# Attention and gated FFN in one kernel: two head groups of the second 512 queries taken ahead, K and Q fillers at half the rate, the first FFN 43 steps later

## The chip, the cores and the metric

The kernel runs on one core of a Trainium2 chip. The metric is the time of one execution on the device in microseconds (us), the median of several runs. The core has four engines that matter here: PE multiplies matrices, ACT evaluates functions such as exp, DVE does elementwise work, SP only issues DMAs. Each engine works through its own instructions in program order.

## What is computed

One transformer layer for 2048 tokens of width 512: a layer norm, attention with 32 heads of width 16, a residual add, a second layer norm, and a gated FFN with 1792 hidden units.

```python
qkv = (x @ wqkv).reshape(B, S, 3, H, Dh)            # x is layernorm(A_x); S=2048, H=32, Dh=16
scores = einsum("bhqd,bhkd->bhqk", q, k) * Dh ** -0.5
o = einsum("bhqk,bhkd->bhqd", softmax(scores), v)
h = A_x + o.reshape(B, S, D) @ wo
hn = layernorm(h)
out = h + (sigmoid(hn @ w_gate) * (hn @ w_up)) @ w_down
```

With 32 heads and 2048 x 2048 scores each, 134 million exponentials are needed. They are the largest piece of work.

## The kernel before, in words

**Chunks, groups, units, steps.** The queries are cut into five chunks c: 0, 1 and 2 of 512 queries, 3 and 4 of 256. The 32 heads are cut into eight head groups g of four heads. A pair (c, g) is worked off over all keys before the next one; the list `qgs` is the order of the pairs, before the change simply c by c, and g by g within c. A unit is a tile of 128 keys by 512 queries of one head (two tiles by 256 queries in chunks 3 and 4); a pair (c, g) of chunks 0 to 2 has 64 units. Three units make a step: three score matmuls on PE (L783) write three PSUM banks `pss`, and one exp on ACT (L794, up to 128x1536) reads them and writes a tile `pt`. There are 683 steps, and two `pss` buffers, so the scores of step i+2 wait until step i has been read. A pair takes 21.3 steps, a chunk of 512 queries 170.7 steps.

**Split steps.** In every fourth step from step 8 to step 680 (`split`), ACT takes only two units (128x1024), and DVE computes the third exp by arithmetic on the bits, in five instructions spread over four steps: L813 (which reads `pss`), L816, L819, L822, L826. I call four steps from one split to the next a cycle. In some cycles, listed in `twice`, a second step is split too. A cycle is also the unit of the timetable: the products with V (`emit_pv`, L864) of four steps come together in one step of the next cycle.

**Score forms.** In the first 44 steps, in odd steps and in `twice` cycles the score matmuls use half the rows of the array each, so that two of them can run side by side (`pairs`); where no filler work is near (`idle`) they do not.

**The filler.** Everything else is one long generator, `filler()`, whose matmuls `emit_fill` slips in behind the scores, at a rate per step (`rate`) and with pauses ("gap", "at", "from"). In order: the nine V tiles left over from the prologue (`fill_v`); for b = 1, 2, 3 the K rows of head groups 2b and 2b+1 (`fill_k`) and the Q rows of chunk 0 for the same groups (`fill_q0`); the Q rows of the other queries, 512 at a time (`fill_q`); then for each chunk c the output projection, the layer norm, gate, up and down products (`ffn_tasks`), each started at a step that depends on the end of the chunk's attention. The filler's products go to one PSUM tile `pm`, so the next block can start only when DVE has emptied it. Up to step 44 (`FIRST`) the rate is that of the V tiles, up to 10 matmuls a cycle; after that it is `RATES[0]`, 2, 2, 0 and 3 in the four steps of a cycle, 0 in the step with three V products.

**What limits the order.** A pair (c, g) needs the K rows of group g//2 and the Q rows of its own queries. `emit_q_rows` and `emit_q_bound` fetch the next pair's Q rows with six DMAs on SP, some four steps before the pair starts. SP also carries the K rows to their places (`k_spread`, two DMAs for each b), the weights (`load_w`: w_gate and w_up from step 44 to 79, w_down from step `GM`+21), the sums of the softmax and back (`emit_norm`: ten small DMAs for each pair), the residual rows and the output.

**Buffers with two lives.** `stg` holds K and the squares of the fillers, `wd` the down weights. Up to step `GM`, three of the seven `pt` buffers lie in `wd`; from `GM` on they lie in `stg` and in the Q rows of chunk 0. The scratch of a second split lies in the buffer `OT` that is free at that time.

**Where each piece falls.** Walking the filler by its rates and pauses, step by step, gives for the kernel before:

| piece of the filler | steps |
|---|---|
| V tiles | 1 to 16 |
| K of b = 1, then Q of chunk 0 for b = 1 | 17 to 31 |
| b = 2 | 31 to 56 |
| b = 3 | 56 to 83 |
| Q of queries 512 to 2047 | 83 to 168 |
| FFN of chunk 0: projection and norm / gate and up / down | 187 to 217 / 217 to 273 / 274 to 320 |
| FFN of chunk 1: the same | 359 to 389 / 389 to 445 / 446 to 492 |
| FFN of chunk 2 | from 523 |
| `twice` cycles of chunk 1's steps, by their second split | 226, 242, 258, 274, 290, 302, 314, 326, 338, 350 |
| `twice` cycles of chunk 2's steps | 402, 418, 434, 450, 458, 470, 482, 494, 506, 518 |

Of the kernel before, what the change touches and what calls it, by code (L numbers as in the profile page):

```python
# [18 lines left out]
def kernel(  # L19
# [13 lines left out]
    S, D = A_x.shape[1], A_x.shape[2]  # L33
# [5 lines left out]
    NG = H // 4  # L39
    FC = F // P  # L40
    QC = 512
    TQ = QC // P
    CHUNKS = [(0, QC), (QC, QC), (2 * QC, QC), (3 * QC, QC // 2), (3 * QC + QC // 2, QC // 2)]
    NC = len(CHUNKS)
    NQC = S // QC
    GU = 3
    CYC = 4
    RATES = ((2.0, 2.0, 0.0, 3.0), (2.0, 2.5, 0.0, 3.0))
    FIRST = 44
    GM = 188  # L50
    G1 = 680
    QS = DH ** -0.5 * 1.4426950408889634 * 2.0 ** 23
    LEAD = 0.106445681
# [14 lines left out]
    def pm_tile():  # L68
        return pmh["pool"].tile([P, 512], FP32, name="pm")
# [27 lines left out]
    QTu = const.tile([P, 4, S], BF16)  # L97
# [65 lines left out]
    def qk_mm(ps, part, b, n, c):  # L163
        w0 = part * D + b * P
        nc.tensor.matmul(ps[:], lhsT=wqkv_sb[:, c, w0:w0 + P], rhs=xnT[:, c, n * QC:(n + 1) * QC],  # L165
                         start=(c == 0), stop=(c == DC - 1))

    def norm_mm(ps, b, sq, start=True, stop=True):
        nc.tensor.matmul(ps[:], lhsT=ones_blk[:, b, :, :].rearrange("p r h -> p (r h)"), rhs=sq,
                         start=start, stop=stop)  # L170
# [21 lines left out]
    def q_root(ps, qc):  # L192
        r = slice(32 * qc, 32 * qc + 32)
        sqrt_bits(y0[r, :], ps[r, :])

    def q_bound(qc, add):
        r = slice(32 * qc, 32 * qc + 32)
        y = y0[r, :].bitcast(FP32)
        if add:
            nc.vector.scalar_tensor_tensor(out=bnd[r, :], in0=y, scalar=nks[r, 0:1], in1=bnd[r, :],  # L200
                                           op0=ALU.mult, op1=ALU.add)
        else:
            nc.vector.tensor_scalar(out=bnd[r, :], in0=y, scalar1=nks[r, 0:1], scalar2=None, op0=ALU.mult)
# [8 lines left out]
        copy(out=Vaug[:, t, :, 0:DH], in_=heads(ps[:]))  # L212

    ready = set()
    qgs = [(c, g) for c in range(NC) for g in range(NG)]

    def emit_q_rows(n):
        c, g = qgs[n]
# [173 lines left out]
    def per_bank(c):  # L392
        return QC // CHUNKS[c][1]

    def n_k(c):
        return NT // per_bank(c)

    units = [(c, g, k, j) for c in range(NC) for g in range(NG) for k in range(n_k(c)) for j in range(4)]
    groups = [units[i:i + GU] for i in range(0, len(units), GU)]
    NS = len(groups)  # L400
    SPC = NS / NQC

    def first_step(c):
        return NS * CHUNKS[c][0] / S if c < NC else NS

    def fill_v(t):
        ps = pm_tile()
        for c in range(DC):  # L410
            yield 1
            v_mm(ps, t, c)
        v_store(t, ps, nc.vector.tensor_copy)
        ready.add(("v", t))
        yield ("gap", 0)

    def squares(src):
        sq = work.tile([P, QC], BF16, name="sq", tag="xn")
        nc.vector.tensor_tensor(out=sq[:], in0=src, in1=src, op=ALU.mult)
        return sq  # L420
# [35 lines left out]
    def q_store(dst, ps):  # L456
        nc.vector.tensor_scalar(out=dst, in0=ps[:], scalar1=QS, scalar2=None, op0=ALU.mult)

    def fill_q0(b):
        ps = pm_tile()  # L460
        for c in range(DC):
            yield 1
            qk_mm(ps, 0, b, 0, c)
        q_store(QTu[:, b, 0:QC], ps)
        sq = squares(QTu[:, b, 0:QC])
        yield ("gap", 2)
        pn = pm_tile()
        yield 1
        norm_mm(pn, b, sq[:])
        q_root(pn, 0)  # L470
        q_bound(0, True)
        ready.add(("q", 0, b))
        ready.add(("b", 0, b))
        yield ("gap", 1)

    def fill_q(qc):
        cols = slice(qc * QC, (qc + 1) * QC)
        sq4 = stages[qc % 2]
        for b in range(4):
            ps = pm_tile()  # L480
            for c in range(DC):
                yield 1
                qk_mm(ps, 0, b, qc, c)
            q_store(QTu[:, b, cols], ps)
            nc.vector.tensor_tensor(out=sq4[:, b * QC:(b + 1) * QC], in0=QTu[:, b, cols], in1=QTu[:, b, cols],
                                    op=ALU.mult)
            ready.add(("q", qc, b))
            yield ("gap", 3)
        yield ("gap", 2)
        pn = pm_tile()  # L490
        for b in range(4):
            yield 1
            norm_mm(pn, b, sq4[:, b * QC:(b + 1) * QC], start=(b == 0), stop=(b == 3))
        q_root(pn, qc)
        q_bound(qc, False)
        for b in range(4):
            ready.add(("b", qc, b))
        yield ("gap", 1)

# [242 lines left out]
    def filler():  # L742
        for t in range(NV0, NT):
            yield from fill_v(t)
        for b in range(1, 4):
            yield from fill_k(b)
            yield from fill_q0(b)
        for qc in range(1, NQC):
            yield from fill_q(qc)
        for c in range(NC - 1):  # L750
            yield ("from", int(first_step(c + 1)) + (11 if c + 3 >= NC else 15))
            yield from ffn_tasks(c)
        yield from wo_early(NC - 1)

    def rate(i):
        if i < FIRST:
            rates = (4.0 if i > 5 else 0.0, 4.0 if i < 6 else 2.0 if i > 16 else 0.0, 0.0, 4.0)
        elif i - i % CYC + 2 in twice:
            rates = (2.0, 2.0, 0.0, 3.0)
        else:  # L760
            rates = RATES[i >= 3 * SPC]
        return (rates[i % CYC], 1.0, 1.0, 0.0)[n_pv.get(i, 0)]

    def emit_scores(i):
        group = groups[i]
        n = len(group)
        pss = pss2[(i + 1) % 2]
        idle = i >= 3 * FIRST and (state["done"] or state["wait"] > i + CYC)
        pairs = i < FIRST or (i % 2 == 1 or i - i % CYC + 2 in twice) and not idle
        order = list(enumerate(group))  # L770
        if pairs and group[0][3] // 2 == group[1][3] // 2:
            order[1:] = order[:0:-1]
        n_of = max(per_bank(u[0]) for u in group)
        parts = [(ui, u, h) for h in range(n_of) for ui, u in order[:2] if h < per_bank(u[0])]
        parts += [(ui, u, h) for ui, u in order[2:] for h in range(per_bank(u[0]))]
        for ui, (c, g, k, j), h in parts:
            n_qg = c * NG + g
            w = CHUNKS[c][1]
            kt = k * per_bank(c) + h
            assert ("k", g // 2) in ready  # L780
            h0 = 64 * (j // 2)
            rows = slice(h0, h0 + 64) if pairs else slice(0, P)
            nc.tensor.matmul(pss[:, ui, h * w:(h + 1) * w], lhsT=KT[rows, g, kt * P:(kt + 1) * P],  # L783
                             rhs=QB[n_qg % 2][rows, j, 0:w], start=True, stop=True,
                             tile_position=(h0, 0) if pairs else None)
        for c, g, k, j in group:
            n_qg = c * NG + g
            if k == (12 if per_bank(c) == 1 else 0) and j == 3 and n_qg + 1 < len(qgs):
                emit_q_rows(n_qg + 1)
                emit_q_bound(n_qg + 1)  # L790
        slot = i % 7
        pt = pt4[slot] if slot < 4 else (pt_early if i < GM else pt_late)[slot - 4]
        na = n - 1 if i in split else n
        ex = nc.scalar.activation(out=pt[:, 0:na, :], in_=pss[:, 0:na, :], func=ACT.Exp, scale=DH ** -0.5 / QS)  # L794
        if na < n:
            scratch = scratch_of(i)
            tc.declare_no_dep(exp_bits(pss[:, na, :], *scratch).ins, ex.ins,
                              reason="both only read, from different banks")
            later(i + 1, lambda: exp_first(*scratch))
            later(i + 2, lambda: exp_second(*scratch))  # L800
            later(i + 3, lambda: exp_third(pt[:, na, :], *scratch))
        for ui, u in enumerate(group):
            p_of[u] = pt[:, ui, :]

    def scratch_of(i):
        if i % CYC:
            flat = OT[(int((i - 20) / SPC) + 1) % 2][:].rearrange("p g q -> p (g q)")
            return (flat[:, 0:2 * QC].bitcast(mybir.dt.int32), flat[:, 2 * QC:4 * QC].bitcast(mybir.dt.int32),
                    flat[:, 4 * QC:6 * QC].bitcast(FP32))
        return early_scratch if i < GM else late_scratch  # L810

# [94 lines left out]
    def load_w():  # L906
# [4 lines left out]
        for f in (0, 7):  # L911
            later(GM + 21 + f // 2, lambda f=f: nc.sync.dma_start(out=wd[:, f:f + 7, :], in_=wd_v[:, f:f + 7, :]))

# [2 lines left out]
    split = set(range(8, G1, CYC))  # L916
    twice = set()
    for qc in range(1, NQC):
        n0 = int(qc * SPC) + 52
        for n in range(n0, min(int((qc + 1) * SPC) + 16, int(first_step(NC - 1)) + 14)):  # L920
            if n % ((4 if n < n0 + 56 else 3) * CYC) == 0:
                twice.add(n + 2)
    split |= twice
# [88 lines left out]
```

## Time and profile before

| what | value |
|---|---|
| median of three runs | 966.0 us (963.1 to 966.93) |
| the profiled execution's own time | 962.96 us |
| its span, first to last instruction | 961.1 us |
| first exp of step 0 starts | 34.24 us after the span's start |
| step 17 / 33 / 185 / 525 starts | 59.28 / 81.12 / 269.98 / 707.67 us |
| DVE busy / POOL busy | 788.1 us (82%) / 41.5 us (4%) |

The starts of steps are the starts of the exps L794 in the timeline of ACT, counted from step 0; a cycle's time is the distance between the starts of steps n and n+4. An exp of 128x1536 is listed with about 1.45 us, but the next one starts 1.33 us after it, since neighbours overlap; busy shares of ACT near 100% mean that there is no gap between them.

### The profile page before, as it was taken

The page shows a single profiled execution, that of the slowest core. Times are in us where ns is not written, and L with a number is a line of the kernel's source. Part 1 is how long each engine was busy: PE and PEld are TensorE (multiplying, and loading weights), DVE is VectorE, ACT ScalarE, POOL GpSimd, SP SyncE. Part 2 cuts the span into 40 slices and gives each one's busy share as a digit, 9 for nine tenths or more (in the row PEclk, how much of TensorE's full clock was granted, in tenths as well). Part 3 has the DMA queues.
Part 4 walks back from the last instruction along what each step waited for, and adds up shares of the span by engine and source line. Part 5 has one row for each costly group of instructions (what it writes and reads, how often), then busy time and mean ns, then how long its engine had stood idle before and what let it go on. Part 6 is the DMA issues. An engine that isn't in the chain of part 4 may idle for free.

```text
span 961.1 us, 17150 instructions
## 1 busy us (share of the span) xinstructions
PE 826.7 (86%) x6327; PEld 337.8 (35%) x6425; DVE 788.1 (82%) x1428; ACT 895.3 (93%) x767; POOL 41.5 (4%) x49
## 2 busy tenths in 40 slices
PE   4887888888788999988788999988788999888998
PEld 2322222222222332222222233222355555455646
DVE  8589998888788888899888888888888788777653
ACT  4789999999999999999999999999998999899872
POOL 4700000000000000000000000000000000000000
PEclk9999999999999999999999999999999999999999
DMA  5001350000013000000011000001011000110010
GB/s 160 21 8 50 114 117 17 16 16 2 16 26 103 16 16 17 19 12 26 14 27 26 16 16 15 14 15 26 16 31 23 16 13 13 27 32 16 9 35 12
DMA packets 37500, 28.38 MB, mean 30 GB/s; under 512 B 17708, under 2 KB 32776, under 8 KB 37416
## 3 DMA queue, kind: packets, MB, share of 16 engines
q1 hardware_dynamic: 35828, 25.71, 10.4%
q10 hardware_dynamic: 1588, 1.58, 0.5%
q8 instruction: 50, 0.82, 0.4%
q14 instruction: 34, 0.28, 0.1%
HBM read 20.31 MB, written 2.61 MB: 24 GB/s over the span
## 4 chain that ended last, share of the span: by engine, by line
PE 40%; DVE 26%; ACT 23%; issue 7%; DMA 3%; SPq 1%; ACTq 0%; DVEq 0%; POOL 0%; POOLq 0%
PE pss L783 20%; ACT pt L794 12%; PE acc L864 8%; PE pm L530 6%; ACT stg L794 4%; ACT wd L794 4%; DVE stg L813 3%; ACT QTu L794 2%; PE pm L546 2%; DVE reg L816 2%; DVE st L139 2%; DVE pt L826 2%; DVE y L822 2%; PE pm L506 2%; DVE reg L543 1%
## 5 line engine op out<-in xcount | busy, mean ns | idle before, releaser
L783 PE MATMUL pss<-QB,KT 64*128 64x512 bf16 (+3 forms) x2542 | 475.8, 336 | 86.9 <-ACT pt L794 43.8
L794 ACT ACTIVATE pt<-pss 128x1536 bf16<-128x1536 f32 (+1 forms) x392 | 501.1, 1363 | 16.3 <-PE pss L783 12.0
L783 PEld LDWEIGHTS <-KT 64*128 64x128 bf16 (+1 forms) x2560 | 181.4, 95 | 345.3 <-issue 232.5
L794 ACT ACTIVATE stg<-pss 128x1536 bf16<-128x1536 f32 (+1 forms) x140 | 183.1, 1355 | 4.6 <-PE pss L783 3.8
L813 DVE TENSOR_SCALAR stg<-pss 128x512 int32<-128x512 f32 x123 | 84.8, 689 | 69.3 <-PE pss L783 53.0
L864 PE MATMUL acc<-pt,Vaug 128*17 128x512 bf16 (+1 forms) x1471 | 112.5, 338 | 4.5 <-DVE xs_all L838 3.2
L794 ACT ACTIVATE wd<-pss 128x1536 bf16<-128x1536 f32 (+1 forms) x80 | 103.8, 1390 | 2.7 <-PE pss L783 2.4
L794 ACT ACTIVATE QTu<-pss 128x1024 bf16<-128x1024 f32 (+1 forms) x71 | 95.5, 1345 | 1.7 <-PE pss L783 1.2
L819 DVE SCALAR_TENSOR_TENSOR y<-reg 128x512 f32<-128x512 f32 x123 | 85.2, 692 | 4.2
L822 DVE SCALAR_TENSOR_TENSOR y<-y,reg 128x512 f32<-128x512 f32 x123 | 84.2, 684 | 1.1
L864 PEld LDWEIGHTS <-Vaug 128*17 128x17 bf16 x2560 | 50.4, 89 | 96.1 <-issue 80.8
L530 PE MATMUL pm<-reg,reg 128*128 128x512 bf16 (+1 forms) x252 | 55.6, 333 | 8.7 <-DVE reg L543 6.6
L530 PE MATMUL pm<-reg,wu 128*128 128x512 bf16 (+1 forms) x280 | 58.1, 338 | 1.5 <-ACT sg L535 1.2
L546 PE MATMUL pm<-wd,reg 128*128 128x512 bf16 x173 | 51.2, 381 | 5.7 <-issue 2.9
L146 POOL TENSOR_TENSOR rs<-ve,pw_neg 128x1 f32<-128x1 f32 (+1 forms) x24 | 17.7, 736 | 888.9 <-DVE ve L144 758.0
L816 DVE TENSOR_SCALAR reg<-stg 128x512 int32<-128x512 int32 x123 | 52.0, 423 | 2.0
L864 PE MATMUL acc<-stg,Vaug 128*17 128x256 bf16 (+1 forms) x564 | 50.6, 326 | 0.6 <-DVE stg L826 0.4
L543 DVE SCALAR_TENSOR_TENSOR reg<-sg,pm 128x512 bf16<-128x512 f32 x56 | 38.2, 682 | 13.9 <-PE pm L530 13.5
L826 DVE SCALAR_TENSOR_TENSOR pt<-y,stg 128x512 bf16<-128x512 f32 x70 | 47.8, 683 | 1.8
L535 ACT ACTIVATE sg<-pm 128x512 f32<-128x512 f32 x56 | 35.6, 637 | 10.1 <-PE pm L530 9.8
L813 DVE TENSOR_SCALAR wd<-pss 128x512 int32<-128x512 f32 x45 | 30.9, 688 | 15.9 <-PE pss L783 14.9
L165 PE MATMUL pm<-reg 128*128 128x512 bf16 x112 | 35.6, 391 | 2.2 <-issue 0.8
(129 smaller groups left out, 707.5 us busy)
## 6 DMA issues: line engine op xcount, KB each, us to landing
rb_all<-rd SPq DMA_DIRECT2D x96, 64.0 KB
reg<-in_A_x_dram SPq DMA_DIRECT2D x8, 256.0 KB
xr<-in_A_x_dram SPq DMA_DIRECT2D x16, 128.0 KB
out_dram<-ob SPq DMA_DIRECT2D x15, 128.0 KB
rb_all<-rd SPq DMA_DIRECT2D x60, 32.0 KB
KT<-stg SPq DMA_DIRECT2D x7, 256.0 KB
reg<-in_B_w_gate_dram SPq DMA_DIRECT2D x4, 448.0 KB
wu<-in_B_w_up_dram SPq DMA_DIRECT2D x4, 448.0 KB
```

The costliest lines, as they stand in the source:

```text
L165: nc.tensor.matmul(ps[:], lhsT=wqkv_sb[:, c, w0:w0 + P], rhs=xnT[:, c, n * QC:(n + 1) * QC], start=(c == 0), stop=(c == DC - 1))
L530: nc.tensor.matmul(ps[:, i * w:(i + 1) * w], lhsT=wt[:, c, f * P:(f + 1) * P], rhs=hnT[:, c, 0:w], start=(c == 0), stop=(c == DC - 1))
L543: nc.vector.scalar_tensor_tensor(out=out, in0=a, scalar=1.0, in1=b, op0=ALU.add, op1=ALU.mult)
L546: nc.tensor.matmul(ps[:], lhsT=hT[:, f, tt * P:(tt + 1) * P], rhs=wd[:, f, :], start=(f == 0), stop=(f == FC - 1))
L783: nc.tensor.matmul(pss[:, ui, h * w:(h + 1) * w], lhsT=KT[rows, g, kt * P:(kt + 1) * P], rhs=QB[n_qg % 2][rows, j, 0:w], start=True, stop= ...
L794: ex = nc.scalar.activation(out=pt[:, 0:na, :], in_=pss[:, 0:na, :], func=ACT.Exp, scale=DH ** -0.5 / QS)
L813: return nc.vector.tensor_scalar(out=e_bits, in0=src, scalar1=ONE_BITS, scalar2=0.0, op0=ALU.add, op1=ALU.max)
L816: nc.vector.tensor_scalar(out=e_man, in0=e_bits, scalar1=0x7FFFFF, scalar2=-0x40800000, op0=ALU.bitwise_and, op1=ALU.bitwise_or)
L819: nc.vector.scalar_tensor_tensor(out=e_pol, in0=m, scalar=PA, in1=m, op0=ALU.add, op1=ALU.mult)
L822: nc.vector.scalar_tensor_tensor(out=e_pol, in0=e_pol, scalar=PB, in1=e_man.bitcast(FP32), op0=ALU.add, op1=ALU.mult)
L826: nc.vector.scalar_tensor_tensor(out=dst, in0=e_pol, scalar=PC, in1=e_bits.bitcast(FP32), op0=ALU.add, op1=ALU.mult)
L864: nc.tensor.matmul(acc[32 * j:32 * j + VW, 0:w], lhsT=Vaug[:, kt, 4 * g + j, :], rhs=p[:, h * w:(h + 1) * w], start=(kt == 0), stop=(kt == ...
```

## The change

The order of the pairs becomes (0,0), (0,1), (1,0), (1,1), (0,2) to (0,7), (1,2) to (1,7), and then chunks 2, 3 and 4 as before. Chunk 0 so ends at step 213.3 in place of 170.7, chunk 1 at step 341.3 as before. K of b = 1 is first needed in step 85 in place of 42. The V rate ends at step 24 (`VF`), while 44 (`FIRST`) still rules the score forms, and after it the rates are 2, 1, 0 and 1 in place of 2, 2, 0 and 3. The filler computes Q of the second 512 queries for b = 0 right behind the V tiles; `fill_q` of these queries leaves that block out, and its pause behind each block is 1 step in place of 3. `GM` and with it the change of buffers and the load of w_down come 28 steps later. The starts of the FFNs and of the `twice` cycles go by the step in which a chunk really ends (`end_step`).

```diff
-    RATES = ((2.0, 2.0, 0.0, 3.0), (2.0, 2.5, 0.0, 3.0))
+    RATES = ((2.0, 1.0, 0.0, 1.0), (2.0, 2.5, 0.0, 3.0))
     FIRST = 44
-    GM = 188
+    GM = 216
+    VF = 24
...
-    qgs = [(c, g) for c in range(NC) for g in range(NG)]
+    qgs = [(c, g) for g0, g1 in ((0, 2), (2, NG)) for c in range(2) for g in range(g0, g1)]
+    qgs += [(c, g) for c in range(2, NC) for g in range(NG)]
+    at_qg = {qg: n for n, qg in enumerate(qgs)}
...
-    units = [(c, g, k, j) for c in range(NC) for g in range(NG) for k in range(n_k(c)) for j in range(4)]
+    units = [(c, g, k, j) for c, g in qgs for k in range(n_k(c)) for j in range(4)]
...
-    def first_step(c):
-        return NS * CHUNKS[c][0] / S if c < NC else NS
+    def end_step(c):
+        return (max(n for n, u in enumerate(units) if u[0] == c) + 1) / GU
...
-    def fill_q0(b):
+    def fill_q1(qc, b):
+        cols = slice(qc * QC, (qc + 1) * QC)
...
-        q_bound(0, True)
-        ready.add(("q", 0, b))
-        ready.add(("b", 0, b))
+        q_bound(qc, b > 0)
+        ready.add(("q", qc, b))
+        ready.add(("b", qc, b))
...
-    def fill_q(qc):
+    def fill_q(qc, b0):
...
-        for b in range(4):
+        for b in range(b0, 4):
...
-            yield ("gap", 3)
+            yield ("gap", 1)
...
     def filler():
         for t in range(NV0, NT):
             yield from fill_v(t)
+        yield from fill_q1(1, 0)
         for b in range(1, 4):
             yield from fill_k(b)
-            yield from fill_q0(b)
+            yield from fill_q1(0, b)
         for qc in range(1, NQC):
-            yield from fill_q(qc)
+            yield from fill_q(qc, int(qc == 1))
         for c in range(NC - 1):
-            yield ("from", int(first_step(c + 1)) + (11 if c + 3 >= NC else 15))
+            yield ("from", int(end_step(c)) + (11 if c + 3 >= NC else 15))
             yield from ffn_tasks(c)
...
     def rate(i):
-        if i < FIRST:
+        if i < VF:
...
-        n0 = int(qc * SPC) + 52
-        for n in range(n0, min(int((qc + 1) * SPC) + 16, int(first_step(NC - 1)) + 14)):
+        n0 = int(end_step(qc - 1)) + 52
+        for n in range(n0, min(int((qc + 1) * SPC) + 16, int(end_step(NC - 2)) + 14)):
```

The same walk for the changed order gives these steps:

| piece of the filler | steps before | steps after |
|---|---|---|
| V tiles | 1 to 16 | 1 to 16 |
| Q of the second 512 queries, b = 0 | in the 83 to 168 below | 17 to 23 |
| K and Q of b = 1 | 17 to 31 | 23 to 51 |
| K and Q of b = 2 | 31 to 56 | 51 to 83 |
| K and Q of b = 3 | 56 to 83 | 83 to 113 |
| the rest of Q | 83 to 168 | 113 to 181 |
| FFN of chunk 0: projection and norm / gate and up / down | 187 to 217 / 217 to 273 / 274 to 320 | 231 to 261 / 261 to 317 / 318 to 364 |
| FFN of chunk 1: the same | 359 to 389 / 389 to 445 / 446 to 492 | 371 to 401 / 401 to 457 / 458 to 504 |
| FFN of chunk 2 | from 523 | from 523 |
| `twice` of chunk 1's steps | 226, 242, 258, 274, 290, 302, 314, 326, 338, 350 | 274, 290, 306, 322, 326, 338, 350 |
| `twice` of chunk 2's steps | ten, from 402 to 518 | the same |

More of the change, by code (lines that the diff above doesn't have):

```diff
@@ L462, in fill_q0 @@
             yield 1
-            qk_mm(ps, 0, b, 0, c)
-        q_store(QTu[:, b, 0:QC], ps)
-        sq = squares(QTu[:, b, 0:QC])
+            qk_mm(ps, 0, b, qc, c)
+        q_store(QTu[:, b, cols], ps)
+        sq = squares(QTu[:, b, cols])
         yield ("gap", 2)
@@ L469, in fill_q0 @@
         norm_mm(pn, b, sq[:])
-        q_root(pn, 0)
-        q_bound(0, True)
-        ready.add(("q", 0, b))
-        ready.add(("b", 0, b))
+        q_root(pn, qc)
+        q_bound(qc, b > 0)
+        ready.add(("q", qc, b))
+        ready.add(("b", qc, b))
         yield ("gap", 1)
-    def fill_q(qc):
+    def fill_q(qc, b0):
         cols = slice(qc * QC, (qc + 1) * QC)
         sq4 = stages[qc % 2]
-        for b in range(4):
+        for b in range(b0, 4):
             ps = pm_tile()
@@ L487, in fill_q @@
             ready.add(("q", qc, b))
-            yield ("gap", 3)
+            yield ("gap", 1)
         yield ("gap", 2)
         pn = pm_tile()
-        for b in range(4):
+        for b in range(b0, 4):
             yield 1
-            norm_mm(pn, b, sq4[:, b * QC:(b + 1) * QC], start=(b == 0), stop=(b == 3))
+            norm_mm(pn, b, sq4[:, b * QC:(b + 1) * QC], start=(b == b0), stop=(b == 3))
         q_root(pn, qc)
-        q_bound(qc, False)
-        for b in range(4):
+        q_bound(qc, b0 > 0)
+        for b in range(b0, 4):
             ready.add(("b", qc, b))
@@ L776, in emit_scores @@
         for ui, (c, g, k, j), h in parts:
-            n_qg = c * NG + g
+            n_qg = at_qg[c, g]
             w = CHUNKS[c][1]
@@ L786, in emit_scores @@
         for c, g, k, j in group:
-            n_qg = c * NG + g
+            n_qg = at_qg[c, g]
             if k == (12 if per_bank(c) == 1 else 0) and j == 3 and n_qg + 1 < len(qgs):
```

## The prediction

> **What bounds the kernel now.** First the page: which engine is nearest to full.
>
> ```profile
> PE 826.7 (86%) x6327; PEld 337.8 (35%) x6425; DVE 788.1 (82%) x1428; ACT 895.3 (93%) x767; POOL 41.5 (4%) x49
> PEclk9999999999999999999999999999999999999999
> ```
>
> ACT, mostly with exps, and the clock of PE is full everywhere. Averages hide stages, so next the busy time by stage: the last V tiles and the first K (steps 17 to 32), the other K and Q fillers (33 to 184), the FFN of chunk 0 in its down part (273 to 320), the steps without filler behind it (321 to 356), the down part of chunk 1 (445 to 492).
>
> ```profile
> core 0: us, PE busy (x) PEld busy (x) DVE busy (x) ACT busy (x) POOL busy (x), PEclk, DMA share, GB/s
> 59.30:81.10 21.80, 18.36 (x122) 5.04 (x122) 20.32 (x42) 20.26 (x16) 0.00 (x0) 1.00 0.11 26
> 81.10:270.00 188.90, 155.62 (x1005) 48.75 (x1023) 160.63 (x283) 188.57 (x154) 0.00 (x0) 1.00 0.17 44
> 386.80:445.60 58.80, 53.20 (x340) 16.61 (x345) 53.13 (x90) 58.34 (x49) 0.00 (x0) 1.00 0.08 20
> 445.60:490.30 44.70, 34.49 (x212) 11.48 (x216) 39.46 (x67) 44.29 (x38) 0.00 (x0) 1.00 0.09 22
> 607.00:668.00 61.00, 52.70 (x340) 16.21 (x345) 53.66 (x91) 58.78 (x50) 0.00 (x0) 1.00 0.08 19
> ```
>
> The reader is to see that where the K and Q fillers run, ACT is idle for 0.33 us of 188.9. The fillers that the change slows are already hidden there; only the first row (1.54 us idle) and the down part of chunk 1 (2.22 us) have gaps. Third, the exps in the first of these, in ACT's timeline:
>
> ```profile
> 70.03 1.45 ACT L794 ACTIVATE wd<-pss 128x1536 bf16<-128x1536 f32 x1 [0.47 <-PE pss L783]
> 71.64 2.79 ACT L794 ACTIVATE wd<-pss 128x1536 bf16<-128x1536 f32 x2 [0.17 <-PE pss L783]
> 76.21 4.13 ACT L794 ACTIVATE pt<-pss 128x1536 bf16<-128x1536 f32 x3 [0.68 <-PE pss L783]
> ```
>
> ACT waits for scores that PE brings late, behind filler matmuls. Last, what happens behind two second splits eight steps apart (450 and 458), from PE's and ACT's timelines:
>
> ```profile
> 627.16 0.82 PE L783 MATMUL pss<-QB,KT 128*128 128x512 bf16 x3 [0.83 <-DVE stg L813]
> 629.09 0.38 PE L864 MATMUL acc<-pt,Vaug 128*17 128x512 bf16 x1 [0.56 <-DVE pt L826]
> 630.10 3.82 ACT L794 ACTIVATE pt<-pss 128x1536 bf16<-128x1536 f32 x3 [0.57 <-DVE y L819]
> ```
>
> DVE, behind with its exps, reads `pss` late, PE waits for it, and ACT for PE. What DVE pays for one third of a split step is in the groups of the page:
>
> ```profile
> L813 DVE TENSOR_SCALAR stg<-pss 128x512 int32<-128x512 f32 x123 | 84.8, 689 | 69.3 <-PE pss L783 53.0
> L819 DVE SCALAR_TENSOR_TENSOR y<-reg 128x512 f32<-128x512 f32 x123 | 85.2, 692 | 4.2
> L822 DVE SCALAR_TENSOR_TENSOR y<-y,reg 128x512 f32<-128x512 f32 x123 | 84.2, 684 | 1.1
> L816 DVE TENSOR_SCALAR reg<-stg 128x512 int32<-128x512 int32 x123 | 52.0, 423 | 2.0
> L826 DVE SCALAR_TENSOR_TENSOR pt<-y,stg 128x512 bf16<-128x512 f32 x70 | 47.8, 683 | 1.8
> ```
>
> That is 0.689 + 0.423 + 0.692 + 0.684 + 0.683 = 3.17 us. An undisturbed cycle lasts 4.95 us (160.62, 165.56, 170.51: starts of steps 97, 101, 105), so one split fits and two do not.
>
> **The sum, part by part.** Up to step 17 and from step 523 on the two programs order the same work alike; only what lies between counts, 59.28 to 702.75 us.
>
> (a) Steps 17 to 32. Before, the four cycles carry 8, 8, 7 and 1 filler matmuls and last 5.21, 5.54, 6.18 and 4.91 us, 21.84 in all. After, they carry 4, 1, 4 and 4. DVE loses the tail of K here (L443 0.68 us, and six small ones) and two of four K blocks (0.69 + 0.43 us each), and gains one Q block (0.68 + 0.43) with its bound (0.68 + 0.74). Cycles with up to 5 matmuls ran in 4.92 to 4.95 us (steps 33 to 45), so I take 5.1 + 5.0 + 5.1 + 4.95 = 20.15: **-1.7 us**; bounds -2.0 (four times 4.95) and -0.3 (only half of the 0.68 us ahead of step 29 goes).
>
> (b) Steps 33 to 184. The name "half rate" misleads: the same 132 matmuls took steps 17 to 168 and take 17 to 181, for the old pauses already held them back. 38 cycles last 188.86 us, 0.76 over 38 x 4.95. The new fillers hold one K block back behind another as before: **0**; bounds -0.7 and +1.0 (four more cycles like the 5.22 of step 77). What is hidden here is hidden by the exp; without that cover 132 matmuls of 0.38 us would cost 50 us. Q of (1, 0) is emitted at 23 and fetched at 38, needed at 42.7; K of b = 1 has 40 steps, over 50 us.
>
> (c) Cycles without filler are 17 before (9 from 321, 8 from 493) and 17 after (11 from 185, one at 365, 5 from 505). Before, with six second splits, they last 44.67 + 39.73 = 84.40, 4.96 each: the split saves 0.13 to 0.42 of 4.95, and the next cycles give it back (5.08 to 5.40). After, twelve are like those of steps 173 to 188 (5.09, 4.91, 4.92, 4.95: mean 4.97) and the last five like before (24.41): 84.0, **-0.4**; bounds -1.0 and +1.0 (all twelve at 4.92, or 5.08).
>
> (d) The down part of chunk 0. Before, second splits at 274, 290, 302 and 314, 58.83 us. After, at 322, 326, 338 and 350, relative to the part 5, 9, 21 and 33 steps in; 322 and 326 are neighbours. Splits at 320, 322, 324, 326, 328 and 332 are 6 x 3.17 = 19.0 us of DVE; add the copy of `acc` at 326 (0.69), a reciprocal (0.25) and an output row (0.68): 20.6 in four cycles that want 4 x 4.92 - 0.8 = 18.9. By the same count the pair 450 and 458 had 21.3 against 18.9 and its four cycles took 20.56: 1.7 us lost of 2.4 over. So 1.0 here, more because the burst is tighter, and the smooth pair 274 and 290 is gone: **+1.2**; bounds 0 and +3.3 (the whole excess of the three cycles from 320 on, 17.5 against 14.2). Queued behind the late L813 are the other DVE exps; for them waits PE with the V products, in order ahead of the next scores.
>
> (e) The rest of the FFNs moves as a whole by 44 and 12 steps, a multiple of four, with its loads of rows, transposes, stores and the down weights (needed 44 steps later, loaded 28 later). FFN 0 and FFN 1 cost alike today though they lie differently to the pairs' ends: projection 40.5 and 40.7, gate and up 76.3 and 76.0. **0**; bounds -1.5 and +1.5 (most of the 2.15 between the down parts).
>
> (f) SP. Every pair issues the same 6 and 10 DMAs, in another order. The K rows of b = 2 (two DMAs of 256 KB) now enter SP's queue at step 69, one step ahead of the sums of a pair. If these come late, DVE stands at the reciprocal L849, with its exps behind it. The trace has four such waits, together 6.6 us, the longest 2.5. **0**; bounds 0 and +2.5.
>
> Sum: -1.7 - 0.4 + 1.2 = **-0.9 us**. The profiled execution took 962.96 us, so 962.1 for one like it; it lies 3.0 under the median, which I carry over: 966.0 - 0.9 = **965.1 us**. About 0.5% (4.8 us) is what a measurement of this kernel can tell from no change.
>
> **Rivals.**
>
> *A tired PE.* With the fillers thin PE idles more, and its clock could fall. No filler at all ran at 445.6 to 490.3 with PE busy 77% and a clock of 1.00. At half the clock those 77% would be 154% of a cycle, for 49 cycles from step 33: 0.54 x 4.96 x 49 = 131 us more, 1096. [...] Chance 0.01.
>
> *DVE falls behind for good* (the other side: slower). Place: step 322, price by the bounds of (d) plus the surplus of chunk 1's down part over chunk 0's, 2.15, which would then be paid in both: 3.3 + 2.15, less 2.1 saved, +3.4 us, or +5.9 with (f): 969.4 to 972, I say 970.5. It decides once these stalls exceed 2.1 us. For it: the 6.05 and 6.13 us cycles behind 458 and 470. Against: 302 and 314 cost almost nothing. Chance 0.18.
>
> *The stalls of DVE's second splits mostly vanish* because the pairs' ends now meet the FFNs elsewhere. The cycles behind them in gate and up lost 6.07, 5.69, 6.21 against 5.37 (1.9 us), in chunk 1's down part 5.30, 6.05, 6.13, 5.39 against 4.92 (3.2). With (a) and (c) that is -7.2: 959. Against: three of the four remaining spacings stay. Chance 0.17.
>
> *Slower fillers do not help at all,* the waits of (a) being DVE's and not the fillers': (a) is 0, 966.8. Against: PE's matmuls stand ahead of the late scores. Chance 0.05.
>
> **From these to the numbers.** The forecast has 0.59 and 962.5 to 968 as its own range. Faster by over 0.5%: nearly all of the third rival, 0.15. Slower: two thirds of the second, the first, and a little of (b) and (f): 0.16. The rest, 0.69, is within. The range takes in 960 (the better part of the gain) to 970.5.
>
> **What would show it.** Steps 17 to 33 in about 20.2 us; steps 33 to 185 in 188 to 190; exps near 4.95 us a cycle up to step 228; behind step 326 a cycle over 5.5 us with PE waiting for L813; chunk 2's end (step 523 on) as before. I am wrong if (a) stays at 21 us or more, if ACT is idle for over 2 us between steps 33 and 228, or if the cycles behind 326 do not stretch.

## The result

The changed kernel takes 967.38 us, the median of 20 runs (965.56 to 968.84), against 964.25 (962.2 to 967.31) for the kernel before, also 20 runs: a ratio of 1.0032, 95% interval 1.0023 to 1.004. It is slower by some 3.1 us, where 0.9 us less was forecast. The profiled executions took 966.92 and 962.96 us, with spans of 965.1 and 961.1.

The page of the changed kernel, its first line:

```profile
PE 831.2 (86%) x6327; PEld 336.3 (35%) x6425; DVE 779.8 (81%) x1415; ACT 896.9 (93%) x767; POOL 41.5 (4%) x49
```

ACT has 1.6 us more to do, DVE 8.3 less: three exps went from DVE to ACT. That is less than the time lost, so the rest must be waits. The stages, as shown of before: steps 17 to 32, 33 to 184, the steps without filler (now 185 to 228), the down part of chunk 0 (317 to 364), that of chunk 1 (457 to 504). PEclk is the share of its full clock that PE was granted. In the changed kernel the scores stand in L788, the exps in L799, the first instruction of DVE's exp in L818 and its second in L821; runs that add `spread()` have these five lines later.

```profile
core 0: us, PE busy (x) PEld busy (x) DVE busy (x) ACT busy (x) POOL busy (x), PEclk, DMA share, GB/s
58.00:77.70 19.70, 15.59 (x108) 4.37 (x108) 16.78 (x30) 19.70 (x16) 0.00 (x0) 1.00 0.02 3
77.70:270.60 192.90, 163.99 (x1018) 48.99 (x1037) 165.74 (x298) 189.05 (x153) 0.00 (x0) 0.99 0.17 45
270.60:326.50 55.90, 42.62 (x260) 13.97 (x264) 37.28 (x61) 55.30 (x45) 0.00 (x0) 1.00 0.06 16
443.20:503.90 60.70, 52.94 (x340) 16.35 (x345) 53.42 (x90) 58.72 (x50) 0.00 (x0) 1.00 0.07 19
626.00:687.00 61.00, 52.98 (x340) 16.41 (x345) 53.80 (x92) 58.73 (x49) 0.00 (x0) 1.00 0.09 24
```

In the first row ACT has no gap left, as was hoped. In the second, where before it stood for 0.33 us of 188.9, it now stands for 3.85 of 192.9, and PE's clock is no longer whole. Taken from the starts of the exps, the same pieces of work compare like this (us):

| piece | before | after | difference | forecast |
|---|---|---|---|---|
| steps 0 to 16 | 25.04 | 23.72 | -1.32 | 0 |
| steps 17 to 32 (a) | 21.84 | 19.76 | -2.09 | -1.7 |
| steps 33 to 184 (b, f) | 188.86 | 192.90 | +4.05 | 0 |
| 17 cycles without filler (c) | 84.39 | 85.62 | +1.23 | -0.4 |
| chunk 0, down (d) | 58.84 | 60.70 | +1.86 | +1.2 |
| the other FFN parts of chunks 0 and 1 (e) | 294.45 | 294.87 | +0.4 | 0 |
| from step 525 | 253.40 | 253.33 | -0.1 | 0 |

Of the 4.05 in the third line one cycle alone, that from step 105, has 3.36: 8.31 us in place of 4.95. SP's and PE's timelines of the changed kernel show what stands in it, ACT's what follows:

```profile
164.85 1.20 SPq L207 DMA_DIRECT2D KT<-stg  x2
166.14 3.12 SPq L226 DMA_DIRECT2D QB<-QTu  x4
169.31 1.27 SPq L236 DMA_DIRECT2D QB<-bnd  x2
```

```profile
171.11 0.38 PE L788 MATMUL pss<-QB,KT 128*128 128x512 bf16 x1 [2.39 <-DMA QB<-bnd]
```

```profile
171.58 4.06 ACT L799 ACTIVATE pt<-pss 128x1536 bf16<-128x1536 f32 x3 [2.16 <-PE pss L788]
176.23 1.45 ACT L799 ACTIVATE wd<-pss 128x1536 bf16<-128x1536 f32 x1 [0.59 <-PE pss L788]
```

PE reaches the first score of pair (0,3), in step 106, and its Q rows are not there. SP issued them at 166.14, right behind the two DMAs with the K rows of b = 3, for which SP had stood 5.8 us waiting for `stg` from DVE. The second gap of ACT, 0.59 us, is another matter; the stretches of 2 us around it:

```profile
168.00:170.00 2.00, 0.59 (x2) 0.10 (x1) 1.90 (x5) 1.42 (x2) 0.00 (x0) 1.00 0.22 61
170.00:172.00 2.00, 0.89 (x13) 0.31 (x13) 0.79 (x2) 0.42 (x1) 0.00 (x0) 1.00 0.03 7
172.00:174.00 2.00, 2.00 (x15) 0.59 (x8) 0.66 (x5) 1.90 (x2) 0.00 (x0) 0.60 0.03 8
174.00:176.00 2.00, 2.00 (x7) 0.32 (x5) 1.65 (x5) 1.60 (x2) 0.00 (x0) 0.55 0.00 0
176.00:178.00 2.00, 2.00 (x16) 0.62 (x16) 0.81 (x2) 1.77 (x2) 0.00 (x0) 1.00 0.00 0
```

After the standstill PEclk, the third number from the right, is 0.60 and 0.55 in two stretches, 4 us in all, with PE busy all the time: the wait is paid twice, first as a wait, then as slow matmuls.

### The profile page after: what moved, and what is told of

It reads as the page before. It is cut to its first block, busy times and chain, and to the rows that moved or that the text cites. A ratio compares the mean times of both kernels' runs of the same rounds, so it can differ in the third digit from the quotient of the medians.

```text
span 965.1 us, 17138 instructions
## 1 busy us (share of the span) xinstructions
PE 831.2 (86%) x6327; PEld 336.3 (35%) x6425; DVE 779.8 (81%) x1415; ACT 896.9 (93%) x767; POOL 41.5 (4%) x49
## 4 chain that ended last, share of the span: by engine, by line
PE 41%; DVE 26%; ACT 24%; issue 6%; DMA 2%; SPq 0%; ACTq 0%; DVEq 0%; POOL 0%; POOLq 0%
PE pss L788 20%; ACT pt L799 13%; PE acc L869 8%; PE pm L534 6%; ACT stg L799 4%; ACT wd L799 4%; DVE stg L818 3%; PE pm L550 2%; PE pm L510 2%; ACT QTu L799 2%; DVE pt L831 2%; DVE reg L821 2%; DVE st L140 2%; DVE y L827 2%; DVE reg L547 2%
## 5 line engine op out<-in xcount | busy, mean ns | idle before, releaser
L788 PE MATMUL pss<-QB,KT 64*128 64x512 bf16 (+3 forms) x2538 | 474.9, 337 | 87.1 <-ACT pt L799 41.0
L799 ACT ACTIVATE pt<-pss 128x1536 bf16<-128x1536 f32 (+1 forms) x392 | 501.5, 1365 | 17.7 <-PE pss L788 13.9
L788 PEld LDWEIGHTS <-KT 128*128 128x128 bf16 (+1 forms) x2560 | 181.4, 95 | 339.6 <-issue 236.9
L799 ACT ACTIVATE stg<-pss 128x1536 bf16<-128x1536 f32 (+1 forms) x132 | 172.7, 1358 | 5.1 <-PE pss L788 3.2
L818 DVE TENSOR_SCALAR stg<-pss 128x512 int32<-128x512 f32 x116 | 80.0, 690 | 73.3 <-PE pss L788 62.0
L799 ACT ACTIVATE wd<-pss 128x1536 bf16<-128x1536 f32 (+1 forms) x92 | 119.2, 1387 | 2.3 <-PE pss L788 1.7
L799 ACT ACTIVATE QTu<-pss 128x1024 bf16<-128x1024 f32 (+1 forms) x67 | 91.0, 1358 | 2.2 <-PE pss L788 1.5
L824 DVE SCALAR_TENSOR_TENSOR y<-reg 128x512 f32<-128x512 f32 x116 | 80.3, 693 | 4.0
L827 DVE SCALAR_TENSOR_TENSOR y<-y,reg 128x512 f32<-128x512 f32 x116 | 79.5, 685 | 1.0
L818 DVE TENSOR_SCALAR wd<-pss 128x512 int32<-128x512 f32 x52 | 35.9, 690 | 26.3 <-PE pss L788 24.7
L821 DVE TENSOR_SCALAR reg<-stg 128x512 int32<-128x512 int32 x116 | 49.1, 424 | 2.0
L166 PE MATMUL pm<-reg 128*128 128x512 bf16 x115 | 38.7, 388 | 1.3 <-DVE stg L433 0.7
```

The costliest lines, as they stand in the source:

```text
L818: return nc.vector.tensor_scalar(out=e_bits, in0=src, scalar1=ONE_BITS, scalar2=0.0, op0=ALU.add, op1=ALU.max)
L821: nc.vector.tensor_scalar(out=e_man, in0=e_bits, scalar1=0x7FFFFF, scalar2=-0x40800000, op0=ALU.bitwise_and, op1=ALU.bitwise_or)
L824: nc.vector.scalar_tensor_tensor(out=e_pol, in0=m, scalar=PA, in1=m, op0=ALU.add, op1=ALU.mult)
L827: nc.vector.scalar_tensor_tensor(out=e_pol, in0=e_pol, scalar=PB, in1=e_man.bitcast(FP32), op0=ALU.add, op1=ALU.mult)
```

## The experiments

### Where the K rows stand in SP's queue

Theory: the Q rows stand behind a DMA that waits for DVE. Three kernels move that DMA in three ways. The first issues it two steps later:

```diff
-        for g in (2 * b, 2 * b + 1):
-            k_spread(ku, g, slice(0, S), nc.sync)
+        def spread():
+            for g in (2 * b, 2 * b + 1):
+                k_spread(ku, g, slice(0, S), nc.sync)
+        if b == 3:
+            later(103, spread)
+        else:
+            spread()
```

> The changed kernel, with the two DMAs that spread the K rows of b = 3 issued at step 103 in place of 101, so behind the Q rows of pair (0,3) in SP's queue and not ahead of them. Theory (head of SP's queue: the Q rows stand behind a DMA that waits for DVE): the 2.39 us wait of PE for QB is gone, the cycle from step 105 lasts 4.95 us in place of 8.31, the granted clock is 1.000 in place of 0.998, the span is 965.1 - 3.4 = 961.7 us. Rival (PE's clock falls because the fillers are thin, and the late scores follow from that): the clock still dips near 172 us after the span's start and the cycle stays over 6 us.

Measured: 963.49 us, ratio 0.9994 (0.9985 to 1.0003) to the kernel before, span 961.6. SP's timeline of this kernel:

```profile
159.30 2.45 SPq L226 DMA_DIRECT2D QB<-QTu  x4
161.79 1.25 SPq L236 DMA_DIRECT2D QB<-bnd  x2
165.11 1.19 SPq L207 DMA_DIRECT2D KT<-stg  x2
```

With nothing that waits ahead of them, SP issues the Q rows at 159.30, 6.8 us earlier than in the changed kernel, though their place in the program is the same. The cycle from step 105 lasts 4.95 us, steps 101 to 141 take 49.49 in place of 52.78. The median is 3.9 us lower; 3.4 of it is this cycle, the wait and the slow clock behind it. What did not come as expected is a clock of 1.000 in the profiled execution, which had its dip elsewhere (below); four of the ten runs had 1.000, and none of the changed kernel's twenty.

The second issues them from POOL:

```diff
-            k_spread(ku, g, slice(0, S), nc.sync)
+            k_spread(ku, g, slice(0, S), nc.gpsimd if b == 3 else nc.sync)
```

> The changed kernel, with the same two DMAs issued at the same step, but on POOL's queue in place of SP's. Theory (head of SP's queue): the Q rows no longer stand behind them, the cycle from step 105 lasts 4.95 to 5.3 us, and the span is 961.7 to 962.5. Rival (the DMA engines: 512 KB of K rows take the Q rows' bandwidth, whatever the queue): the wait for QB stays over 1.5 us and the cycle over 6.5.

Measured: 963.55 us, ratio 0.9997 (0.9986 to 1.0008); the cycle from step 105 lasts 4.95 us. SP now issues the Q rows at 160.51, and the K rows wait for DVE on POOL's queue:

```profile
166.85 1.21 POOL L207 DMA_DIRECT2D KT<-stg  x2 [117.82 <-DVE stg L434]
```

So the queue's order is what made the Q rows late. Whether 512 KB of K rows in flight would also slow the Q rows is not settled by this, since they no longer meet; in the changed kernel the four issues took 3.12 us against 2.46 here, so at most 0.7 us of the issue is of that kind.

The third keeps SP and takes back the rates:

```diff
-    RATES = ((2.0, 1.0, 0.0, 1.0), (2.0, 2.5, 0.0, 3.0))
+    RATES = ((2.0, 2.0, 0.0, 3.0), (2.0, 2.5, 0.0, 3.0))
```

> The changed kernel with the old rates 2, 2, 0, 3 from step 24 on: the order of the pairs, the later FFN and everything else stay. The K rows of b = 3 are then spread at step 87, 15 steps ahead of the Q rows of pair (0,3). Theory (the half rate matters by where it puts that DMA): the cycle from step 105 lasts 4.95 us, steps 33 to 185 take 189 to 190 us in place of 192.9, the clock is 1.000; steps 17 to 33 rise from 19.76 to 20 to 20.6; the span is 962 to 963. Rival (the new order of the pairs is what makes the Q rows late): the wait for QB stays near 2.4 us.

Measured: 965.98 us, ratio 1.0022 (1.0012 to 1.0032), span 964.6, so 1.6 above the expected end. The wait is gone (cycle 105 at 4.95, clock 1.000): it is the half rate, not the order of the pairs, that put the K rows at step 101. But steps 0 to 16 took 25.04 again, which had not been thought of, and steps 33 to 184 1.5 us more than in e1_k3_later.

### The neighbours 322 and 326

DVE's, PE's and ACT's timelines of the changed kernel behind the two second splits:

```profile
458.70 0.68 DVE L818 TENSOR_SCALAR stg<-pss 128x512 int32<-128x512 f32 x1
```

```profile
459.44 0.82 PE L788 MATMUL pss<-QB,KT 128*128 128x512 bf16 x3 [1.26 <-DVE stg L818]
```

```profile
456.08 1.45 ACT L799 ACTIVATE stg<-pss 128x1536 bf16<-128x1536 f32 x1 [0.89 <-DVE y L824]
460.36 1.45 ACT L799 ACTIVATE pt<-pss 128x1536 bf16<-128x1536 f32 x1 [0.57 <-PE pss L788]
```

DVE reads the bank for step 328 at 458.70, PE has waited 1.26 us to write it, ACT 0.57 us for PE: the chain that the prediction described. The cycles from 325 and 329 take 5.59 and 6.30 us.

```diff
+    twice.discard(322)
     split |= twice
```

> The changed kernel without the second split at step 322, so that 326 has no neighbour; ACT does one unit more. Theory (DVE's exps pile up behind 322 and 326): the cycles from 325 and 329, 5.59 and 6.30 us, become 4.9 and 5.3 or less, the one from 321 rises from 4.63 to 4.95, the down part of chunk 0 (steps 317 to 365) falls from 60.7 to about 59.2, the span by 1.4. Rival (the part is slower for its place against the pairs' ends, whose copy of acc falls on step 326): the part stays over 60.3.

Measured: 965.91 us, 1.5 below the changed kernel; ratio to before 1.0017 (1.0007 to 1.0027). The three cycles from 321 last 4.95, 4.78 and 4.98 in place of 4.63, 5.59 and 6.30, 1.8 us less. Where the two cycles had three gaps, ACT's timeline has one unbroken run:

```profile
457.02 5.06 ACT L799 ACTIVATE pt<-pss 128x1536 bf16<-128x1536 f32 x4
```

### Steps 0 to 16, which nobody had touched

Up to step 17 the two programs give PE, ACT and DVE the same work, yet the changed one is 1.32 us ahead. Before, DVE's and POOL's timelines:

```profile
46.60 2.25 DVE L816 TENSOR_SCALAR reg<-wd 128x512 int32<-128x512 int32 x1
```

```profile
45.03 1.79 POOL L954 MEMSET wo_pad<- 128x2048 bf16 x1
46.77 1.79 POOL L433 MEMSET KT<- 128x2048 bf16 x1
48.63 0.37 POOL L959 CAST ident_f<-ident_bf 128x128 f32<-128x128 bf16 x1
```

After, the same instruction of DVE, and POOL:

```profile
46.60 0.51 DVE L821 TENSOR_SCALAR reg<-wd 128x512 int32<-128x512 int32 x1
```

```profile
43.28 3.54 POOL L436 MEMSET KT<- 128x2048 bf16 x2
46.88 0.37 POOL L964 CAST ident_f<-ident_bf 128x128 f32<-128x128 bf16 x1
47.19 1.80 POOL L436 MEMSET KT<- 128x2048 bf16 x1
```

POOL works off its few instructions far ahead of the steps in which they are emitted: the last memset of `KT`, emitted in step 97, ran at 47.19 us, while step 97 began at 158.02. With the half rate this memset is emitted behind the copy of the identity (steps 97 and 90; before 68 and 90). DVE's instruction, 0.42 us on average, starts at 46.60 with a memset in progress in both kernels. Before, a second memset followed, and L816 ended at 48.85, 0.29 us behind that second one; after, the copy followed, and it ended at 47.11, 0.29 us behind the memset in progress. Whether it is the next instruction of POOL that decides, two runs of the kernel before are to show:

```diff
-        later(90, lambda: nc.gpsimd.tensor_copy(out=ident_f[:], in_=ident_bf[:]))
+        later(62, lambda: nc.gpsimd.tensor_copy(out=ident_f[:], in_=ident_bf[:]))
```

> The kernel before, with one small POOL copy (of the identity, 0.37 us) put ahead of the last two memsets in POOL's order, so that the last memset of KT starts some 0.4 us later, as in the changed kernel. Theory (the 1.3 us by which the changed kernel reaches step 17 earlier come from POOL: a memset of 1.79 us that starts at 46.77 holds up DVE's L816, 2.25 us in place of 0.42): L816 at 46.60 takes 0.4 to 0.5 us, the cycle from step 9 falls from 6.83 to 5.5, steps 0 to 17 from 25.04 to 23.7, the median by 1.3. Rival (chance of one execution, or the order of the pairs): the cycle stays at 6.8.

Measured: 964.63 us, ratio 1.0003 (0.999 to 1.0015), and L816 at 46.69 took 2.50 us. The copy now ran at 45.13, one memset too early, and DVE met two memsets as before (45.36 and 47.10). That a later start of the last memset is enough was wrong. With `later(66, ...)` the copy goes between the last two, so that no second memset is right behind the one in progress at 46.60:

> The kernel before, with the same POOL copy now between the last two memsets (the place before was one memset too early: DVE's L816 then met the next memset). [...] Rival (steps 0 to 17 differ for another reason): L816 stays at 2.2 us or more.

Measured: 962.91 us, ratio 0.9992 (0.9979 to 1.0004), span 959.7. L816 takes 0.51 us in place of 2.25, steps 0 to 16 take 23.72 in place of 25.04; every stage from step 17 on lasts as before to within 0.1 us. The trace settles the 1.32 us, a side effect of the rates on POOL's order; the interval of the ratio still holds 1.

The other profiles agree: in e4_pool_order (2.50 us) and e7_old_rates (2.27), with two memsets back to back, L816 ends 0.29 us behind the second, in e11_copy_between (0.51) 0.29 us behind the one in progress. What holds DVE up in that time is not shown.

### Two repairs together, and what the score forms do

e1_k3_later and e3_no_322 in one kernel:

> The changed kernel with both repairs: the K rows of b = 3 spread at step 103, no second split at 322. Theory (the two costs add): the wait for QB is gone, the cycles behind 322 and 326 are below 5.1, the median is 963.5 - 1.5 = 962.0, a ratio of 0.998 to the kernel before. Rival (one of the two gains was chance, or the time goes to the clock): 963 to 964.

Measured: 962.95 us, ratio 0.9988 (0.9975 to 1.0), span 960.3. In the traces the gains add (the cycles behind 326 at 4.9, no wait for QB); of the median's expected 1.5 us only 0.5 is seen, less than these runs can tell apart.

The 17 cycles without filler had cost 1.23 us more and not 0.4 less: most of those from step 185 on last 5.09 us. There the scores are unpaired.

```diff
-        idle = i >= 3 * FIRST and (state["done"] or state["wait"] > i + CYC)
+        idle = False and (state["done"] or state["wait"] > i + CYC)
```

> As e8_later_no_322, with the score matmuls of odd steps paired also where no filler is near (steps 184 to 223, 352 to 364, 504 to 518). Theory (these cycles last 5.09 us and not 4.95 because unpaired scores, 0.81 us in place of 0.61, make PE late behind the V products): they fall to 4.92 to 4.95, steps 185 to 229 from 55.9 to 54.3, the median by 1.5 to 2. Rival (the thinner PE loses its clock there): the granted clock falls to 0.99 or less with dips between 270 and 320 us, matmuls of 0.38 us take 0.60, and the time does not fall.

Measured: 961.66 us, ratio 0.9977 (0.996 to 0.9995). Theory and rival are both right. Most undisturbed cycles from step 189 on fall to 4.90 to 4.95. But of the five dips of the profiled execution (mean clock 0.991) two fall into this stretch, and steps 185 to 228 took 56.83 us, more than the 55.87 of the changed kernel. Parts of these two, by stretches of 4 us:

```profile
270.00:274.00 4.00, 3.18 (x21) 0.56 (x11) 1.87 (x4) 3.10 (x3) 0.00 (x0) 0.76 0.00 0
298.00:302.00 4.00, 3.48 (x20) 0.84 (x20) 2.96 (x5) 3.88 (x4) 0.00 (x0) 0.65 0.01 2
```

Another, 0.69 from 226 to 230 us, is no work of this edit: it lies at step 153, where the scores are as in e8_later_no_322, and e12_fewer_splits below has one at the same place. The runs say more than one profile: the ten mean clocks are 0.991 to 0.998, four of them 0.991, against 0.995 to 1.000 in e8_later_no_322. So the form that looks wasteful held the clock better in these runs. In time the two are not told apart: the ten runs here took 960.4 to 965.9 us, those of e8_later_no_322 961.3 to 965.5. The opposite, more PE work in steps 17 to 43, on e8_later_no_322:

```diff
-        pairs = i < FIRST or (i % 2 == 1 or i - i % CYC + 2 in twice) and not idle
+        pairs = i < 17 or (i % 2 == 1 or i - i % CYC + 2 in twice) and not idle
```

> As e8_later_no_322, with the score matmuls of even steps from 17 to 43 unpaired, so that PE has more to do (0.81 us a step in place of 0.61) while the fillers are thin. Theory (thin fillers let the clock fall near 68 us after the span's start in some executions: 0.38 us matmuls took 0.61 in the profiles of e1_k3_later and e2_k3_pool, and the cycle from step 25 took 5.87 and 7.16 us in place of 4.93): the clock is 1.000 in nearly all runs, no run's cycle at step 25 is stretched, the median is 0.5 to 1 us below that of e8_later_no_322. Rival (PE is full and more work makes it late): cycles from 17 to 44 grow over 5.1 us and the median rises.

Measured: 963.31 us, ratio 0.9989 (0.9974 to 1.0004): no gain. The profiled execution had a clock of 1.000 and step 25 unstretched, but of ten runs only four had 1.000, against three of e8_later_no_322. More PE work in these steps does not decide it; why the clock dips in one execution and not in the next stays open.

### Fewer second splits

In e8_later_no_322, after most second splits, the next cycle loses more than ACT has saved. This takes nine more away:

```diff
-    twice.discard(322)
+    twice -= {290, 322, 402, 418, 450, 458, 470, 506, 578, 610}
     split |= twice
```

> As e8_later_no_322, without the second splits at 290, 402, 418, 450, 458, 470, 506, 578 and 610, each of which is followed by a cycle of 5.8 to 7.1 us. ACT does nine units more. Theory (DVE, behind after a second split, holds up the scores of the next cycle by more than ACT has saved): by the rows of e8_later_no_322, the pairs of cycles 289 and 293, 401 and 405, and so on, fall from 5.03 + 6.07 to 2 x 5.37, from 4.61 + 6.13 to 2 x 4.92; in all 5 to 6 us, the median is 957 to 958, ratio 0.993. Rival (ACT is full, each unit given back costs 0.42 us, and the late scores have another cause): 963 + 9 x 0.42 = 966.7, or no change.

Measured: 960.28 us, ratio 0.996 (0.9946 to 0.9973). The cycles do what was said where a split stood alone (5.03 + 6.07 became 2 x 5.37, 4.61 + 6.13 became 4.95 + 5.22), but the pair behind 610 did not fall, 12.69 and now 12.79: its waits have another cause, not looked for. Half of the expected gain came. The last run asks whether the new order of the pairs has a share in it; it is e11_copy_between, without ten second splits:

```diff
+    twice -= {226, 258, 402, 418, 450, 458, 470, 494, 578, 610}
     split |= twice
```

> The kernel before with the POOL copy of e11_copy_between and without ten second splits (226, 258, 402, 418, 450, 458, 470, 494, 578, 610), so without anything of the change. Theory (what e12_fewer_splits gained comes from the second splits and from POOL's order, and the new order of the pairs itself is worth about the 2.1 us of steps 17 to 33): 960.3 + 2 = 962 us, ratio 0.997 to 0.9985, 1 to 2.5 us above e12_fewer_splits. Rival (the new order of the pairs carries the gain): 964, no better than before.

Measured: 959.58 us, ratio 0.9949 (0.9931 to 0.9967): not above e12_fewer_splits, as the theory had it, nor at 964, as the rival had it, but level with e12_fewer_splits, and with the lowest median of this study. It keeps three second splits more than e12_fewer_splits, so the two are no clean pair; but no gain of the new order is left to be seen.

## Why the prediction was wrong

**The step that failed is (f)**, "SP. Every pair issues the same 6 and 10 DMAs, in another order": priced 0. It looked for the K rows of b = 2 at step 69 ahead of a pair's sums; that cost nothing, steps 61 to 101 take 49.71 us in both kernels. The K rows that mattered are those of b = 3: spread at step 101, with the Q rows of pair (0,3) fetched at 102 and needed at 106.7. Both numbers were to be had from the same walk through the filler that gave 69. Before, the spreads stood 14, 12 and 9 steps ahead of the next fetch, after 19, 12 and 1. The wait of 2.39 us lies within the bound of 2.5 that was given there, but its cost, 3.36, does not, since the clock fell behind it. Without it the change is 0.6 us faster than before (e1_k3_later), which these runs cannot tell from none; 0.9 had been forecast.

That e1_k3_later comes so close to the forecast is luck. It holds the 1.32 us of POOL's order, which nobody had forecast; without them it would be some 0.7 us slower than before, an estimate. In the profiled executions, (a) to (e) add up to +2.1 us where -0.9 was forecast, and (c) alone is 1.6 of the difference. In e7_old_rates, with neither the wait nor POOL's gain and a clock of 1.000, the span is 3.5 us above that of before. Luck, too, is that 967.38 lies within the forecast's 962.5 to 968: that range hung on 966.0, a median of three runs, and 20 runs of the kernel before gave 964.25.

**(a) was right** in place and nearly in size: -2.09 for -1.7. No run separates PE's fewer filler matmuls from DVE's lighter work in these steps. In e1_k3_later it was -1.09 and in e2_k3_pool +0.11, with the clock at fault (0.78 and 0.79, and 0.70 and 0.50, from 66 to 70 and 70 to 74 us) and not the fillers.

**(b)**: beside the wait, 0.7 us, within its bounds, and nearly all of it in the cycle from step 53, 5.70 us. There DVE stood 0.73 us at the reciprocal for the sums of a pair, the very wait that (f) had described. It comes and goes: of the eight profiles with the new rates five have that cycle at 5.32 to 5.70 us, while in e3_no_322, the same program up to there, DVE did not wait; before, the cycle took 4.92. Why is not shown.

**(c) had the wrong sign**: +1.23 for -0.4, and over its upper bound of +1.0, twelve cycles at 5.08. It took the four cycles of steps 173 to 188 as the type of a cycle without filler. Only two of them, from 173 and 177, lie in unpaired steps as a whole. And it read the cycles of 5.08 to 5.10 us behind the splits of before as giving back what the splits had saved; after, nine cycles without any second split nearby take 5.03 to 5.37, most of them 5.09, and with paired scores most fall to 4.90 to 4.95 (e9_paired_idle). So 5.09 was the plain length of a cycle with unpaired scores.

**(d) was right** in mechanism, place and sign: +1.86 for +1.2, inside 0 to +3.3, and e3_no_322 gives 1.8 back. **(e)** held.

**Work before step 17** was taken as alike because PE, ACT and DVE had the same order; POOL had not, and -1.32 us came unforeseen.

**The rivals.** A PE that loses its clock through thin fillers was given 0.01, since the steps without filler had run at a clock of 1.00 with PE busy 77%. That was one execution, and others have dips without a long wait of PE. The same steps in e1_k3_later, first, and in the changed kernel, in both behind waits of PE of 0.73 and 0.76 us:

```profile
66.00:70.00 4.00, 3.25 (x17) 0.66 (x14) 2.90 (x6) 4.00 (x4) 0.00 (x0) 0.78 0.00 0
70.00:74.00 4.00, 3.57 (x19) 0.67 (x20) 2.67 (x5) 3.33 (x4) 0.00 (x0) 0.79 0.03 4
```

```profile
66.00:70.00 4.00, 3.14 (x22) 0.84 (x22) 3.37 (x7) 4.00 (x4) 0.00 (x0) 1.00 0.00 0
70.00:74.00 4.00, 3.49 (x28) 0.94 (x31) 3.44 (x7) 4.00 (x4) 0.00 (x0) 1.00 0.03 4
```

The two programs differ only from step 101 on, and one has a clock of 0.78. What was wrong is the price, a clock that falls to half for good (131 us). It did fall to half, 0.50 from 70 to 74 us in e2_k3_pool and from 172.5 to 175.5 us in the changed kernel, but only in stretches of up to 8 us; the cycle from step 25 took 0.94 us more in e1_k3_later and 2.2 in e2_k3_pool. Nor are the thin fillers shown to be the cause: with the old rates, e4_pool_order has such a dip in the cycle from step 33 (0.57 from 82 to 86 us). DVE's backlog, the rival on the slower side, is real, but with its 1.86 us alone the change would not have been slower.

## What to carry to other kernels

When a change moves work between queues, walk every in-order queue with the step numbers of both programs and look for a DMA that waits for fresh data just ahead of one that is needed soon; the small engines count like the large ones (here SP's queue cost 3.36 us, POOL's order 1.32). A second engine that takes over work helps only as long as it is not behind itself: look at the cycle after (here 4.63 us, then 5.59 and 6.30). And compare single stages of the trace, since gains of 1 to 2 us and losses of 1 to 4 us cancelled here to a third of a per cent.

## What the hardware showed that was not expected

PE's granted clock differs between executions of one program, in small steps. Of 30 executions of the kernel before, those measured beside e1_k3_later, 5 had a mean clock of 1.000 (median 963.1 us), 2 had 0.999 (963.0), 19 had 0.998 (964.3), 4 had 0.996 (966.0): each 0.002 goes with 1.2 to 1.7 us, and that is most of the spread of these runs. Of the 20 of the changed kernel none had 1.000 and ten had 0.996, which fits a dip behind the wait at step 105 in every execution; the two profiles that have the wait, that of the changed kernel and that of e3_no_322, both show it (0.60 and 0.55 from 172 to 176 us, and 0.60 from 170 to 174). The profile of before shown above was one of the undisturbed ones. In the two profiles with the wait the clock fell behind a standstill of PE: 2.39 us in the changed kernel, and in e3_no_322 within a stretch of 4 us (166 to 170) that had PE busy for 1.49; in e1_k3_later and e2_k3_pool it fell behind waits of 0.73 and 0.76 us. What decides it is not shown.
